# Where PReLU reads its product: PSUM or the scaled copy in SBUF

## The chip, the cores and the metric

The kernel runs on one core of one Trainium2 chip. The metric is the device time of one execution in microseconds. The core's engines are TensorE (PE in the profile; PEld is its weight load), VectorE (DVE), ScalarE (ACT), GpSimd (POOL) and SyncE (SP, which only issues DMAs here). They run side by side; each works through its own instructions in a fixed order and waits on semaphores for the others.

## The reference

An attention over pooled keys and values, and behind it a feed-forward layer with a PReLU:

```python
k_p = k.reshape(B, H, Sp, 8, D).mean(axis=3)          # B 8, H 8, S 576, D 64, Sp 72
v_p = v.reshape(B, H, Sp, 8, D).mean(axis=3)
scores = scale * np.matmul(q, k_p.transpose(0, 1, 3, 2))
attn = softmax(scores)
x = np.matmul(attn, v_p)                               # to 4608 x 512
h = x @ w_in                                           # 512 -> 2048
g = np.maximum(h, 0.0) + alpha * np.minimum(h, 0.0)    # alpha: one per column of h
out = g @ w_out                                        # 2048 -> 512
```

All inputs and outputs are fp32.

## The kernel before

The 4608 tokens are cut into 9 chunks of 512 (`CH`). Each chunk passes through attention (scores, softmax, a transpose by DMA, the product with v), through FFN1 and through FFN2. FFN1 has 16 slices of 128 hidden columns (`NF`), FFN2 has 4 tiles of 128 tokens (`TPC`). To keep the precision of fp32, each operand of a product is split into a high and a low fp16 part and three matmuls are made of one: L766 to L768 in FFN1, L813 to L815 in FFN2.

One slice `f` of FFN1 goes from engine to engine:

1. `ffn1_products` (TensorE): 12 matmuls of 128x512 into one PSUM bank `h`. There are two such banks (`ps_h`, `bufs=2`), so slice f+2 can start only when the bank of slice f has been read for the last time.
2. `ffn1_scaled` (ScalarE, L772): t = h * rp, from PSUM to an fp32 tile in SBUF.
3. `ffn1_prelu` (VectorE, L776): t = max(h * ra, t). It reads h from PSUM and t from SBUF.
4. `ffn1_parts` with l = 0 (ScalarE, L784): the high fp16 part of t.
5. `ffn1_parts` with l = 1 (GpSimd, L787): the low part, t minus the high part; then g is ready for FFN2.

`rp` and `ra` hold one factor per hidden column: rp is a scale with the sign that makes the maximum right, and ra is rp * alpha. `al` holds alpha itself. All three are written once, in the opening stage.

The opening stage (`start`, some 160 us) also loads, scales and splits the weights. It contains chunk 0 with an order on all engines that is written out by a planner (`_Plan`, with ranks in `RK`) and fixed under `manual_schedule`. From chunk 1 on the order on each engine is chosen by the framework's own scheduler, from the order of the program, the dependences between the tiles and a timeline of its own. In the program, the attention of chunk c+1 is spread over the FFN1 slices of chunk c: k and q scales (the small VectorE operations at L212, L217, L233, L238), the split of k and q (L426, L429, L442, L446), softmax (L511 to L547), the transposes, and the sums over 8 values of v on GpSimd (L467). FFN2 steps of the same chunk may run between FFN1 slices as far as their g is ready.

Of the kernel before, what the change touches and what calls it, by code (L numbers as in the profile page):

```python
# [136 lines left out]
def pooled_attention_prelu_ffn(ctx: ExitStack, tc: tile.TileContext, qT, kT, vT, kN, vN, w1, w2, alpha, out):  # L137
# [5 lines left out]
    nc = tc.nc  # L143
# [38 lines left out]
    al = const.tile([P, NF], F32, name="al")  # L182
# [574 lines left out]
    gs, hps, hs = {}, {}, {}  # L757
# [14 lines left out]
        nc.scalar.activation(t, hps[c, f], AF.Copy, scale=rp[:, f:f + 1])  # L772

    def ffn1_prelu(c, f):
        t = hs[c, f]
        nc.vector.scalar_tensor_tensor(out=t, in0=hps.pop((c, f)), scalar=ra[:, f:f + 1], in1=t,  # L776
                                       op0=ALU.mult, op1=ALU.max)

    def ffn1_parts(c, f, l):
# [46 lines left out]
    def start():  # L826
# [35 lines left out]
        for f in range(NF):  # L862
            rank = due[1](f)
            if f:
                x = add("PE", 2.59, lambda f=f: ffn1_products(0, f), wd[1, f], first, rank=rank, take="h")
            else:
                x = wd[1, f]
                for n in range(NK):
                    x = add("PE", 0.64, lambda n=n: ffn1_products(0, 0, slice(n, n + 1)), x, xd[n],
                            rank=rank, take=None if n else "h")  # L870
                first = x
            x = add("ACT", 0.69, lambda f=f: ffn1_scaled(0, f), x, rs[f], rank=rank + RK["sc"], take="f")
            x = add("DVE", 0.76, lambda f=f: ffn1_prelu(0, f), x, rank=rank + RK["pre"], give="h")
            rd.append(x)
            x = add("ACT", 0.62, lambda f=f: ffn1_parts(0, f, 0), x, rank=rank + RK["hi"])
            gd.append(add("Pool", 1.2, lambda f=f: ffn1_parts(0, f, 1), x, rank=rank + RK["lo"], give="f"))
# [34 lines left out]
    for c in range(1, NC):  # L911
        line = _Line()
        if c + 1 < NC:
            attention(line.add, c + 1, _new_b(c + 1), 0.0)
        mixes = 5 * (NPR // 2)
        n = -(-(len(line.ops) - mixes) // (NF - 2))
        for f in range(NF):
            ffn1_products(c, f)
            ffn1_scaled(c, f)
            ffn1_prelu(c, f)  # L920
            ffn1_parts(c, f, 0)
            ffn1_parts(c, f, 1)
            with (tc.issue_after(last["t"].ins), tc.issue_after(last["x"].ins), tc.issue_after(last["xh"].ins),
                  tc.issue_after(last["o"].ins)):
                line.emit(min(n, len(line.ops) - mixes))
        for i in range(TPC):
            ffn2(c, i)
            if i == 1:
                line.emit(mixes)
# [32 lines left out]
```

## Time and profile before

| | |
|---|---|
| median of 3 runs | 902.24 us (900.93 to 907.07) |
| profiled execution | 903.4 us |
| span of its instructions | 901.7 us |
| mean granted TensorE clock | 0.985 |
| TensorE matmul busy | 846.9 us (94% of the span) |
| ScalarE busy | 430.6 us (48%) |
| VectorE busy | 407.2 us (45%) |
| GpSimd busy | 347.8 us (39%) |

A line of the page's groups reads: source line, engine, operation, what it writes and reads by the program's names, shapes, how many; then busy time, mean ns of one, the engine's idle time just before them, and what ended most of it. A line of the waits reads: who waited, on what; total us, times, longest. In the timeline the first number is the start in us from the span's beginning and the second the length in us; rows of one kind that follow each other are merged (x2). Matmuls are pipelined, so that a matmul of 0.38 us is followed by the next after a shorter time.

### The profile page before, as it was taken

How to read it: one execution, taken by the hardware profiler on the slowest of the kernel's cores; microseconds unless marked ns; L12 is line 12 of the kernel's file. 1: busy time of each engine (PE TensorE's matmuls, PEld its weight loads, DVE VectorE, ACT ScalarE, POOL GpSimd, SP SyncE). 2: the span in 40 equal slices, each digit the busy share in tenths (PEclk: the TensorE clock that was granted, in tenths of full speed). 3: DMA queues.
4: the chain of work that ended last, by engine and by line, in shares of the span. 5: the costliest groups of instructions: out<-in, count | busy, mean ns of one | idle time of the engine just before them, and what ended most of it. 6: DMA issues, size and time to landing. Idle time of an engine off the chain costs nothing.

```text
span 901.7 us, 11443 instructions
## 1 busy us (share of the span) xinstructions
PE 846.9 (94%) x4404; PEld 405.8 (45%) x4404; DVE 407.2 (45%) x657; ACT 430.6 (48%) x727; POOL 347.8 (39%) x375
## 2 busy tenths in 40 slices
PE   5779899989898989999989999999989999999998
PEld 4444354444344444454435444544444444444443
DVE  4889895484128520762077116621572145111110
ACT  5899984555324631563246234632464346313330
POOL 1357364376214730564055504640455027302320
PEclk9889999999999999999999999999999999999999
DMA  9686033606210360045012601260115004000000
GB/s 331 218 264 257 25 86 65 198 4 156 87 51 4 71 172 24 27 74 172 24 27 51 172 36 39 48 175 36 39 27 117 36 13 77 18 35 12 1 23 25
DMA packets 93638, 74.73 MB, mean 83 GB/s; under 512 B 77040, under 2 KB 77616, under 8 KB 93584
## 3 DMA queue, kind: packets, MB, share of 16 engines
q1 hardware_dynamic: 93584, 74.01, 29.2%
q8 instruction: 34, 0.56, 0.3%
q14 instruction: 20, 0.16, 0.1%
HBM read 45.10 MB, written 9.44 MB: 60 GB/s over the span
## 4 chain that ended last, share of the span: by engine, by line
PE 65%; DVE 11%; issue 7%; ACT 6%; DMA 6%; POOL 4%; SPq 1%; POOLq 0%; DVEq 0%; ACTq 0%
PE o L813 10%; PE o L814 10%; PE o L815 10%; PE h L766 9%; PE h L767 9%; PE h L768 9%; DMA vraw<-vT_dram 3%; POOL g L787 3%; DVE t L776 2%; DVE e L233 2%; DVE q L446 1%; PE x L609 1%; DMA nat<-kN_dram 1%; SPq L254 1%; ACT q L442 1%
## 5 line engine op out<-in xcount | busy, mean ns | idle before, releaser
L787 POOL TENSOR_TENSOR g<-t,g 128x512 f16<-128x512 f32 x144 | 166.9, 1160 | 397.7 <-ACT g L784 393.4
L776 DVE SCALAR_TENSOR_TENSOR t<-h,m,t 128x512 f32<-128x512 f32 x144 | 107.0, 744 | 308.4 <-ACT t L772 303.7
L766 PE MATMUL h<-x,w 128*128 128x512 f16 x576 | 220.0, 384 | 17.2 <-DVE t L776 13.9
L767 PE MATMUL h<-x,w 128*128 128x512 f16 x576 | 221.2, 384 | 0.0
L768 PE MATMUL h<-x,w 128*128 128x512 f16 x576 | 221.1, 384 | 0.0
L813 PE MATMUL o<-w,g 128*128 128x512 f16 x544 | 206.1, 380 | 10.7 <-POOL g L787 10.5
L814 PE MATMUL o<-w,g 128*128 128x512 f16 x544 | 206.4, 379 | 0.0
L815 PE MATMUL o<-w,g 128*128 128x512 f16 x544 | 204.4, 380 | 0.0
L772 ACT ACTIVATE t<-h,rp 128x512 f32<-128x512 f32 x144 | 97.5, 682 | 117.4 <-PE h L768 96.2
L784 ACT CAST g<-t 128x512 f16<-128x512 f32 x144 | 88.6, 615 | 99.0 <-DVE t L776 98.3
L803 ACT ACTIVATE o<-o,os 128x512 f32<-128x512 f32 x34 | 23.1, 687 | 156.3 <-PE o L815 156.3
L767 PEld LDWEIGHTS <-w 128*128 128x128 f16 x576 | 56.9, 99 | 83.4 <-issue 23.9
L813 PEld LDWEIGHTS <-g 128*128 128x128 f16 x576 | 56.3, 98 | 79.7 <-POOL g L787 13.1
L768 PEld LDWEIGHTS <-w 128*128 128x128 f16 x576 | 57.0, 99 | 69.7 <-issue 3.5
L815 PEld LDWEIGHTS <-g 128*128 128x128 f16 x576 | 56.4, 98 | 67.8 <-issue 0.3
L766 PEld LDWEIGHTS <-w 128*128 128x128 f16 x576 | 56.5, 99 | 65.9 <-issue 4.0
L814 PEld LDWEIGHTS <-g 128*128 128x128 f16 x576 | 56.4, 98 | 65.0 <-issue 0.6
L467 POOL TENSOR_TENSOR vraw<-vraw 72x512 f32<-72x512 f32 (+1 forms) x56 | 53.7, 972 | 43.0 <-DMA vraw<-vT_dram 39.2
L570 DVE SCALAR_TENSOR_TENSOR x<-x,xsc,x 128x512 f16<-128x512 f32 x36 | 26.1, 748 | 65.5 <-ACT x L566 65.5
L536 POOL TENSOR_TENSOR e<-e,sm 128x576 f32<-128x576 f32 x35 | 40.5, 1158 | 34.6 <-DVE sm L534 33.6
L541 ACT CAST apad<-e 128x576 f16<-128x576 f32 x72 | 44.9, 669 | 14.6 <-POOL e L536 12.4
L544 POOL TENSOR_TENSOR apad<-e,apad 128x448 f16<-128x448 f32 x36 | 37.3, 1035 | 17.7 <-ACT apad L541 17.6
(135 smaller groups left out, 840.6 us busy)
## 6 DMA issues: line engine op xcount, KB each, us to landing
w<-w_dram SPq DMA_DIRECT2D x16, 1024.0 KB
out_dram<-o SPq DMA_DIRECT2D x36, 256.0 KB
qraw<-qT_dram SPq DMA_DIRECT2D x17, 512.0 KB
vraw<-vT_dram SPq DMA_DIRECT2D x28, 288.0 KB
kraw<-kT_dram SPq DMA_DIRECT2D x12, 576.0 KB
kq<-kT_dram SPq DMA_DIRECT2D x2, 576.0 KB
nat<-kN_dram SPq DMA_DIRECT2D x2, 512.0 KB
nat<-vN_dram SPq DMA_DIRECT2D x2, 512.0 KB
```

The costliest lines, as they stand in the source:

```text
L467: nc.gpsimd.tensor_tensor(out=o, in0=y, in1=z, op=ALU.add)
L541: x = add("ACT", 0.67, lambda l=l, ap=ap, ev_=ev_: nc.scalar.copy(out=ap[:, l, :, :SP], in_=ev_()), x, *td[i - 2:i - 1], rank=rk)
L766: nc.tensor.matmul(ps, w[:, 1, ks_], x[:, 0], start=(n == 0), stop=False)
L767: nc.tensor.matmul(ps, w[:, 0, ks_], x[:, 1], start=False, stop=False)
L768: nc.tensor.matmul(ps, w[:, 0, ks_], x[:, 0], start=False, stop=(n == NK - 1))
L772: nc.scalar.activation(t, hps[c, f], AF.Copy, scale=rp[:, f:f + 1])
L776: nc.vector.scalar_tensor_tensor(out=t, in0=hps.pop((c, f)), scalar=ra[:, f:f + 1], in1=t, op0=ALU.mult, op1=ALU.max)
L784: nc.scalar.copy(out=g[:, 0], in_=t)
L787: nc.gpsimd.tensor_tensor(out=g[:, 1], in0=t, in1=g[:, 0], op=ALU.subtract)
L813: nc.tensor.matmul(ps, g[:, 1, ts_], w[:, 0], start=(f == 0), stop=False)
L814: nc.tensor.matmul(ps, g[:, 0, ts_], w[:, 1], start=False, stop=False)
L815: nc.tensor.matmul(ps, g[:, 0, ts_], w[:, 0], start=False, stop=(f == NF - 1))
```

## The change

In chunk 0 nothing changes. In chunks 1 to 8 the PReLU multiplies the scaled copy t by alpha instead of multiplying h by rp * alpha: max(t * al, t) with t = h * rp is the same value. The first input of the instruction is then t in SBUF and no longer h in PSUM; both its tensors lie in SBUF, and the scaled copy is the last instruction that reads the bank h.

```diff
     def ffn1_prelu(c, f):
-        t = hs[c, f]
-        nc.vector.scalar_tensor_tensor(out=t, in0=hps.pop((c, f)), scalar=ra[:, f:f + 1], in1=t,
+        t, h = hs[c, f], hps.pop((c, f))
+        nc.vector.scalar_tensor_tensor(out=t, in0=t if c else h, scalar=(al if c else ra)[:, f:f + 1], in1=t,
                                        op0=ALU.mult, op1=ALU.max)
```

## The prediction

> **What bounds the kernel now.** I read the page's busy times first, then its costliest groups, then the waits of TensorE, and then went down to single instructions in the timeline.
>
> ```profile
> PE 846.9 (94%) x4404; PEld 405.8 (45%) x4404; DVE 407.2 (45%) x657; ACT 430.6 (48%) x727; POOL 347.8 (39%) x375
> ...
> L776 DVE SCALAR_TENSOR_TENSOR t<-h,m,t 128x512 f32<-128x512 f32 x144 | 107.0, 744 | 308.4 <-ACT t L772 303.7
> ```
>
> TensorE is busy for 94% of the span; VectorE, which runs the changed PReLU (L776, 144 times 744 ns), has more than half of it free. So the change can pay only where TensorE stands still, or cost only where it makes TensorE stand still. The waits of TensorE from 160 us to the end, that is after the opening stage:
>
> ```profile
> PE h L766 <- DVE t L776: 12.9, 7, 2.6
> PE o L813 <- POOL g L787: 10.5, 6, 3.4
> ```
>
> Columns: total us, times, longest. Seven waits, 12.9 us together, are the first matmul of an FFN1 slice (L766) waiting for a PReLU to give back one of the two h banks. Six more, 10.5 us, are FFN2 waiting for a g from GpSimd. The same view over one chunk at a time (160 to 205 us, then to 300, 390, 480, 570, 660) shows where the seven lie:
>
> ```profile
> PE h L766 <- DVE t L776: 1.6, 1, 1.6
> PE h L766 <- DVE t L776: 2.7, 2, 2.3
> PE h L766 <- DVE t L776: 1.8, 1, 1.8
> PE h L766 <- DVE t L776: 2.6, 1, 2.6
> PE h L766 <- DVE t L776: 1.8, 1, 1.8
> PE h L766 <- DVE t L776: 2.3, 1, 2.3
> ```
>
> One long wait per chunk, always at the same place, some 10 us into FFN1 of chunks 1 to 6; the remaining 0.4 us of the second row is a short one. Here is one of them in the timeline (first start, then length, in us; ScalarE, VectorE, GpSimd, TensorE):
>
> ```profile
> 373.63 2.19 ACT L442 ACTIVATE q<-qraw,s 128x1024 f16<-128x1024 f32 x2
> 375.72 1.24 ACT L772 ACTIVATE t<-h,rp 128x512 f32<-128x512 f32 x2
> ...
> 367.72 1.01 DVE L217 TENSOR_SCALAR pr<-pt 128x3 f32<-128x3 f32 x1
> 368.65 0.74 DVE L776 SCALAR_TENSOR_TENSOR t<-h,m,t 128x512 f32<-128x512 f32 x1
> 369.31 2.79 DVE L233 TENSOR_SCALAR e<-pr 128x3 int32<-128x3 int32 x1
> ...
> 374.81 2.48 DVE L446 SCALAR_TENSOR_TENSOR q<-qraw,s,q 128x1024 f16<-128x1024 f32 x2 [0.37 <-ACT q L442]
> 377.21 0.74 DVE L776 SCALAR_TENSOR_TENSOR t<-h,m,t 128x512 f32<-128x512 f32 x1
> ...
> 367.44 1.84 POOL L467 TENSOR_TENSOR vraw<-vraw 72x512 f32<-72x512 f32 x2
> 369.24 1.15 POOL L787 TENSOR_TENSOR g<-t,g 128x512 f16<-128x512 f32 x1
> 370.35 0.61 POOL L467 TENSOR_TENSOR vraw<-vraw 72x256 f32<-72x256 f32 x1
> 370.92 1.16 POOL L787 TENSOR_TENSOR g<-t,g 128x512 f16<-128x512 f32 x1
> ...
> 375.78 0.38 PE L815 MATMUL o<-w,g 128*128 128x512 f16 x1
> 378.01 0.38 PE L766 MATMUL h<-x,w 128*128 128x512 f16 x1 [1.85 <-DVE t L776]
> 380.59 0.22 PE L209 MATMUL pm<-pd,ones 128*128 128x128 bf16 x1
> ```
>
> The reader is to see the order of events. A tiny VectorE operation on 128x3 (L233) is stretched to 2.79 us while GpSimd runs without a break from 367.44 to 372.08. That holds the scales back, so ScalarE reaches its two q copies late, and the two scaled copies (L772) stand behind those. VectorE then makes the two q products (L446) and only then the PReLU (377.21 to 377.95). TensorE starts at 378.01, straight after it, and the 12 matmuls of the slice last until 380.59: 2.58 us a slice, 0.215 a matmul.
>
> **The change part by part.**
>
> *The early release.* After the change the PReLU no longer reads h, so the last reader of an h bank is the scaled copy on ScalarE. In the rows above the first of the two copies ends half way through the pair, at 375.72 + 0.62 = 376.34, and TensorE's last matmul before the wait is over at 375.78 + 0.38 = 376.16. The wait would shrink from 1.85 us to about 0.25: 377.95 - 376.34 = 1.6 us off. Applied to the five waits of 1.8 to 2.6 us this is 5 x 1.6 = 8.0; the waits of 1.6 and 0.4 us go altogether, 2.0. Sum: **-10.0 us**. Bounds: nothing, if the freed bank is found late for another reason, and -12.9, all seven. What is late next is the scaled copy itself, behind q.
>
> *The clock after a wait.* Behind the 2.6 us wait FFN1 matmuls start 0.42 us apart, twice the 0.215 above:
>
> ```profile
> 471.79 0.63 PE L768 MATMUL h<-x,w 128*128 128x512 f16 x1
> 472.21 0.63 PE L766 MATMUL h<-x,w 128*128 128x512 f16 x1
> ```
>
> The stretches of that chunk and of the one before it (the sixth figure after a stretch's length is the granted clock):
>
> ```profile
> 300.00:390.00 90.00, 85.73 (x450) 40.51 (x448) 35.30 (x56) 38.65 (x63) 35.77 (x40) 1.00 0.28 70
> 390.00:480.00 90.00, 86.30 (x443) 40.61 (x442) 38.09 (x59) 37.14 (x61) 33.68 (x37) 0.98 0.29 74
> ```
>
> The clock is 0.98 in the chunk with the 2.6 us wait, which is 0.02 x 90 = 1.8 us, and 1.00 in the chunk with the 1.85 us one. If the long waits shrink below 1 us, the 1.8 comes back; a second chunk with a wait near that length might give as much. I take **-2**, bounds 0 and -4.
>
> *The PReLU's operands.* It still has 128x512 fp32 elements and one instruction; only in0 moves from PSUM to SBUF. The trace has no such PReLU, but it has neighbours:
>
> ```profile
> L691 DVE SCALAR_TENSOR_TENSOR w<-v,s,w x16: 700/746/1757, 105.1 to 147.1; 128x512 f16<-128x512 f32 x16
> L776 DVE SCALAR_TENSOR_TENSOR t<-h,m,t x144: 692/750/779, 67.6 to 872.7; 128x512 f32<-128x512 f32 x144
> L663 DVE SCALAR_TENSOR_TENSOR v<-w,v x2: 1212/1218/1224, 24.1 to 68.3; 128x1024 int32<-128x1024 int32 x2
> L663 DVE SCALAR_TENSOR_TENSOR v<-w,vw x14: 1208/1214/1247, 51.0 to 144.5; 128x1024 int32<-128x1024 int32 x14
> ```
>
> The same instruction with both tensors in SBUF (L691) has a median of 746 ns, against 750 for the PReLU (min/median/max). With two 32-bit SBUF inputs (L663 from v) it takes 1218 ns per 1024 elements, with one of them in PSUM (from vw) 1214. So the bare cost is unchanged: 0, bounds -50 to +50 ns, hidden under TensorE either way.
>
> *The contention.* The maximum of L691 is 1757 ns, while the PReLU's is 779. The row behind it, and what GpSimd ran at that time:
>
> ```profile
> 118.46 1.76 DVE L691 SCALAR_TENSOR_TENSOR w<-v,s,w 128x512 f16<-128x512 f32 x1
> ```
>
> ```profile
> 117.77 2.91 POOL L467 TENSOR_TENSOR vraw<-vraw 72x512 f32<-72x512 f32 x2 [1.48 <-DMA vraw<-vT_dram]
> ```
>
> With two SBUF inputs the instruction waited about 1.0 us for the GpSimd addition under way, and the two additions, about 1.27 us each when alone (1.84 less 0.61 in the rows above), took 2.91 together, 0.4 us more. The Trainium skill, "SBUF — State Buffer", section "Who interferes with whom", says this in general: a VectorE instruction with two SBUF inputs contends with a GpSimd instruction that reads SBUF, and the second to start waits; one SBUF input does not. It speaks against this change, and the two maxima agree with it. Met at random, a PReLU finds GpSimd at work with its share of a chunk, 35.77 of 90 us, or 0.40, and then waits half a GpSimd operation, 0.58 us: 0.23 us each, 16 x 0.23 = 3.7 us per chunk on an engine that is free for 55 of 90. Only what reaches TensorE counts. That is the stage before the long wait: the PReLU at 368.65 now holds GpSimd's 0.61 us addition by up to 0.74 us, GpSimd's streak ends that much later, and L233 with it. The bounds are +0.7 per chunk, and -2 if L233 gets its turn while GpSimd is held. I take +0.5 x 6 chunks = **+3**, bounds -12 and +4.
>
> *Queues behind it.* ScalarE's cast (L784) waits for the PReLU, and the next scaled copy, which now frees the bank, stands behind that cast:
>
> ```profile
> ACT g L784 <- DVE t L776: 98.3, 101, 2.5
> ```
>
> 101 times ScalarE already stands there. A PReLU that is 0.23 us late passes that on to the copy. The cover is the second bank: one slice of FFN1, 2.58 us. Without cover it would be 96 x 0.23 = 22 us in chunks 1 to 6. I take **+1**. The waits for g are put down to GpSimd's queue, whose own wait there is for the vraw load; the PReLU is long over by then, so I leave those 10.5 us.
>
> Sum: -10 - 2 + 3 + 1 = -8 against the profiled execution's 903.4 us (span 901.7 and 1.7 around it): **895.4, say 895 us**. The median of the three runs, 902.24, is 1.2 lower, so this is -0.8%; about 1% is what a measurement of this kernel can tell from no change. One more uncertainty is in every term: from chunk 1 on, the order on each engine is chosen by the framework from the dependences, and the change alters one. Chunk 0 keeps its order and its PReLU.
>
> **The rivals.**
>
> 1. *No change.* The wait changes hands: the scaled copies stand behind the q copies (2.19 us in the row at 373.63), so TensorE waits for ScalarE instead, or the order just spends the freed bank on running into the g wait sooner. For it: both waits come from a chunk of work that arrives late on in-order engines. Against: in the row the copy ends 1.6 us before the PReLU. -10 is then cancelled: 902. This is also how the change would fail to do what it says.
>
> 2. *Much faster.* With banks free, FFN1 runs through and TensorE keeps FFN2 work in hand for the moment when g is late. Then 12.9 us and, say, half of 10.5 go, with 2 of clock: 903.4 - 20 = 883.
>
> 3. *Slower.* Place: the FFN1 stage of chunks 1 to 6, where GpSimd runs softmax and v sums back to back. Mechanism: a PReLU held behind GpSimd holds the cast, the cast holds the scaled copy, the copy holds the bank. It decides as soon as the hold and what stood there before pass the 2.6 us of the second bank; L233's 2.79 us shows that a streak can do that. Price: the early release gains nothing, and each chunk pays one GpSimd operation (1.16 us) and a third of the clock's 1.8 us: 6 x 1.76 = 10.6, so 914. Against: an instruction of this kind got its turn after one GpSimd operation at 118.46.
>
> 4. *Halved rate.* The Trainium skill, "Vector Engine (DVE) Microarchitecture Reference", section "7. Points that are easy to get wrong", says that this instruction with two non-bf16 SBUF sources runs at half throughput. L663 does not agree (1218 against 1214 ns). As a mechanism here: a PReLU as long as L446's (2.48 / 2 = 1.24 us), +0.5 us each; a chunk's 8 us still lie under TensorE, and about +0.5 per chunk reaches it: 898.
>
> **How the numbers follow.** Forecast 0.40, no change 0.25, much faster 0.15, slower 0.16, halved rate 0.04. Around each I allow 6 us for the new order. The forecast then falls below 893 one time in three, the much faster case always: 0.13 + 0.15, with 0.05 from the others 0.33. Above 911 lie two thirds of the slower case, 0.11, and a little of the others, together 0.14. The rest is 0.53. Leaving out half of the much faster case and half of the slower one gives 882 to 914.
>
> **What would show it.** In the profile after, TensorE's waits on the PReLU should be gone outside chunk 0, with waits of under 1 us on the scaled copy at most; the PReLU's maximum should rise from 779 ns to 1.5 to 2 us with a median near 750; GpSimd's L787 should average more than the 1.15 us of the rows above; the granted clock should be 1.00 in the chunk of 390 to 480. Were the median near 1.2 us, rival 4 holds. If TensorE waits on the scaled copy for as long as it waited on the PReLU, rival 1; if the cast's wait of 98 us rises by tens of us and TensorE's with it, rival 3. An order that moves softmax or v work against FFN1 would make the working wrong, whatever the sign.

## The result, and the profile after

The changed kernel takes 873.38 us (median of 4 runs, 871.39 to 876.16) against 902.62 us: a ratio of 0.967, 95% interval 0.963 to 0.972. Measured again (e11 below) the ratio is 0.966 (0.963 to 0.969). The change is worth 29 us where 8 were forecast, and 873 lies below the range of 882 to 914. One of the ten runs of e1 below, the profiled one, took 1266.6 us at a granted clock of 0.66 and is left out of e1's figures.

TensorE's busy row, and the groups of PReLU and of GpSimd's low part, in the profile after:

```profile
PE 840.7 (96%) x4404; PEld 406.4 (46%) x4404; DVE 425.9 (49%) x657; ACT 428.8 (49%) x727; POOL 367.1 (42%) x375
...
L787 POOL TENSOR_TENSOR g<-t,g 128x512 f16<-128x512 f32 x144 | 174.5, 1213 | 362.1 <-ACT g L784 359.5
L776 DVE SCALAR_TENSOR_TENSOR t<-t,al 128x512 f32<-128x512 f32 x128 | 125.1, 979 | 272.3 <-ACT t L772 261.6
```

PReLU in chunks 1 to 8 became slower, 979 ns on average where it took 744, and GpSimd's L787 too, 1213 ns for 1160. Yet TensorE's waits from 160 us on have nearly gone:

```profile
PE h L766 <- ACT t L772: 2.5, 1, 2.5
PE h L766 <- ACT o L803: 1.4, 1, 1.4
PE o L813 <- ACT o L803: 0.2, 1, 0.2
```

That is the whole list: 4.1 us. Before it was 12.9 + 10.5, and 1.6 in these last two rows as well: 25.0 us. So 20.9 us of the 27.3 by which the span shrank are waits of TensorE, and both kinds have gone, the waits for PReLU and those for g. The clock gives part of the rest. Behind 160 us it drops in three short stretches before and in one after, and is 1.00 between them (the sixth figure behind the length is the granted clock):

```profile
235.00:239.50 4.50, 4.50 (x14) 1.71 (x15) 0.75 (x1) 2.91 (x6) 0.51 (x1) 0.62 0.31 117
283.00:287.50 4.50, 4.50 (x24) 2.29 (x22) 1.29 (x5) 1.50 (x3) 2.25 (x3) 0.62 0.00 0
471.00:475.00 4.00, 4.00 (x16) 1.66 (x15) 0.66 (x2) 1.05 (x3) 2.31 (x2) 0.57 0.02 4
```

```profile
190.00:194.50 4.50, 3.97 (x12) 1.44 (x12) 3.30 (x5) 2.67 (x5) 1.73 (x2) 0.62 0.02 4
```

Each costs some 1.7 us (0.38 of 4.5, 0.43 of 4.0), so the clock gives 5.1 - 1.7 = 3.4 us. Each follows a long wait: 3.4 us for g and 2.3 and 2.6 us for PReLU before, 2.5 us for the scaled copy after. Not every wait of that length does it: behind 2.4 us for g, at 332 us before, the clock stays at 1.00. Waits and clock make 24.3 of the 27.3 us; the other 3 were not traced.

What the prediction did not have in its sum is the second thing that changed: the order on the engines. FFN2 matmuls fill the gaps of FFN1. The first of their three lines, in FFN1 of chunk 3, before (356 to 416.3 us) and after (345 to 399.5 us):

```profile
L813 PE MATMUL o<-w,g 128*128 128x512 f16 x23 | 8.7, 379 | 0.0
```

```profile
L813 PE MATMUL o<-w,g 128*128 128x512 f16 x17 | 6.4, 379 | 0.0
```

Counted in TensorE's order of instructions over all three lines, out of 192 FFN2 matmuls per chunk, 62 to 78 came before the end of the chunk's FFN1, in chunks 1 to 8; after the change it is 46 to 51, and 66 in the last. More FFN2 work is in hand when FFN1 ends.

### The profile page after: what moved, and what is told of

The parts are those of the page before. It is cut to its first block, busy times and chain, and to the rows that moved or that the text cites. A ratio compares the mean times of both kernels' runs of the same rounds, so it can differ in the third digit from the quotient of the medians.

```text
span 874.4 us, 11435 instructions
## 1 busy us (share of the span) xinstructions
PE 840.7 (96%) x4404; PEld 406.4 (46%) x4404; DVE 425.9 (49%) x657; ACT 428.8 (49%) x727; POOL 367.1 (42%) x375
## 4 chain that ended last, share of the span: by engine, by line
PE 85%; DVE 6%; ACT 4%; DMA 2%; issue 1%; SPq 1%; POOL 0%; ACTq 0%; POOLq 0%
PE o L813 13%; PE o L815 13%; PE o L814 13%; PE h L766 13%; PE h L768 13%; PE h L767 13%; PE x L609 2%; DMA nat<-kN_dram 1%; PE s L598 1%; PE s L599 1%; DVE t L776 1%; PE s L600 1%; DMA qraw<-qT_dram 1%; DVE m L242 1%; PE h L815 1%
## 5 line engine op out<-in xcount | busy, mean ns | idle before, releaser
L787 POOL TENSOR_TENSOR g<-t,g 128x512 f16<-128x512 f32 x144 | 174.5, 1213 | 362.1 <-ACT g L784 359.5
L776 DVE SCALAR_TENSOR_TENSOR t<-t,al 128x512 f32<-128x512 f32 x128 | 125.1, 979 | 272.3 <-ACT t L772 261.6
L813 PE MATMUL o<-w,g 128*128 128x512 f16 x544 | 205.8, 379 | 0.3 <-ACT o L803 0.2
L784 ACT CAST g<-t 128x512 f16<-128x512 f32 x144 | 88.6, 615 | 99.9 <-DVE t L776 99.5
L813 PEld LDWEIGHTS <-g 128*128 128x128 f16 x576 | 56.3, 98 | 68.6 <-issue 1.5
L467 POOL TENSOR_TENSOR vraw<-vraw 72x512 f32<-72x512 f32 (+1 forms) x56 | 55.5, 1008 | 46.8 <-DMA vraw<-vT_dram 32.4
L536 POOL TENSOR_TENSOR e<-e,sm 128x576 f32<-128x576 f32 x35 | 44.5, 1273 | 19.6 <-DVE sm L534 19.6
L544 POOL TENSOR_TENSOR apad<-e,apad 128x448 f16<-128x448 f32 x36 | 39.4, 1095 | 14.8 <-ACT apad L541 14.6
```

Source lines behind the costliest of these rows:

```text
L467: nc.gpsimd.tensor_tensor(out=o, in0=y, in1=z, op=ALU.add)
L776: nc.vector.scalar_tensor_tensor(out=t, in0=t if c else h, scalar=(al if c else ra)[:, f:f + 1], in1=t, op0=ALU.mult, op1=ALU.max)
L784: nc.scalar.copy(out=g[:, 0], in_=t)
L787: nc.gpsimd.tensor_tensor(out=g[:, 1], in0=t, in1=g[:, 0], op=ALU.subtract)
L813: nc.tensor.matmul(ps, g[:, 1, ts_], w[:, 0], start=(f == 0), stop=False)
```

## The experiments

Two theories. **R**: the early release of the bank saves the time, as in the prediction's sum. **O**: the new order saves it; on the chip itself the early release matters little. To tell them apart, I took the order apart from the operands. The instructions have the same numbers in both kernels, so an order can be laid down as edges of issue order, which make no engine wait for another (shortened, marked by "..."; e1 lays down the list "PE" alone):

```diff
+ORDER = {"PE": "...", "DVE": "...", "Activation": "...", "Pool": "..."}   # numbers of instructions, in order
+def pin_order(nc, tc):
+    made = {i.name: i for i in nc.cur_bb.bb.instructions}
+    for ids in ...:
+        for a, b in zip(ids, ids[1:]):
+            tc.add_manual_dep(made[f"I-{b}"], f"I-{a}", mybir.DependencyInfo(
+                mybir.DependencyClass.NoSync, mybir.DependencyReason.DATA), reason="order")
```

**e1, new operands in the old order.** The changed kernel with TensorE's order of before laid down; the other engines then had their old orders too.

> The changed PReLU, but every engine works through chunks 1 to 8 in the order that it had before the change. The h bank is free after the scaled copy, nothing else differs. Theory R (the early release as such pays, by the prediction's sum): the waits for PReLU fall from 12.9 us to under 4, the 10.5 us of waits for g stay, about 893 to 896 us. Theory O (the new order pays, the bank's earlier release on the chip matters little): 898 to 904 us.

Measured: 0.999 (0.996 to 1.002), 902.08 us (median of nine). With the old order the change does nothing that can be measured.

**e2, old operands in the new order.** The kernel before with the order of the changed one laid down on four engines.

> The old PReLU, which reads h from PSUM and holds the bank, but every engine works through chunks 1 to 8 in the order of the changed kernel. Theory O: the waits for g vanish, since FFN1 runs ahead and FFN2 work is left for when g is late; some waits for PReLU remain; 876 to 886 us. Theory R: without the early release TensorE waits in this order for PReLU in most slices of FFN1, 895 us or more.

Measured: 873.50 us, 0.967 (0.964 to 0.971), a little better than even theory O had it. The order alone gives the whole gain, with the PReLU that holds the bank. TensorE's waits from 160 us on (L869 is the first FFN1 line here, L879 PReLU):

```profile
PE h L869 <- DVE t L879: 2.0, 2, 1.0
PE h L869 <- ACT o L906: 1.4, 1, 1.4
```

Waits for PReLU fall from 12.9 to 2.0 us although it still gives back the bank; no wait for g is left. Theory R is out as an account of the 29 us.

**e3, two SBUF inputs, bank held, old order.** The changed kernel in the old order, and behind the PReLU:

```diff
...
+        if c:
+            nc.vector.tensor_copy(out=held, in_=h[:, :1])     # held: 128x1 in SBUF
```

> The changed PReLU with the order of before on every engine, and behind each PReLU VectorE copies one column of h, so that the bank is held as long as before. What is left of the change is that PReLU has two SBUF inputs and can meet GpSimd. The prediction's contention terms, with no gain against them: 903 to 908 us. If contention costs nothing that reaches TensorE: 901 to 904 us. PReLU's mean should be near 980 ns, as in the changed kernel.

Measured: 920.58 us, 1.019 (1.014 to 1.024), 17 us more. The cost is far above the forecast, although PReLU's mean is 831 ns and not the 980 expected. The waits (L896 is GpSimd's low part, L886 the copy that holds the bank):

```profile
PE o L922 <- POOL g L896: 18.0, 7, 4.8
PE h L873 <- DVE held L886: 17.0, 8, 3.1
```

Both kinds have grown, 10.5 to 18.0 and 12.9 to 17.0. The copy itself takes 0.15 us each time and can have a part in both; what it adds was not measured apart, so the 17 us are not the price of the contention alone.

**e4, one SBUF input, new order.** The changed kernel in its own order, with

```diff
+            nc.vector.tensor_reduce(out=t, in_=t.rearrange("p (a b) -> p a b", b=1), axis=AX.X, op=ALU.max)
```

in place of PReLU in chunks 1 to 8; the product with alpha and the maximum are left out there.

> The order of the changed kernel on every engine, early release too, but in chunks 1 to 8 the PReLU is replaced by a VectorE reduction over groups of one element, from t to t, with one SBUF input and the same 128x512 elements: the product with alpha and the maximum are left out there. It should not meet GpSimd: near 750 ns with a maximum under 0.8 us. If contention costs the changed kernel what the prediction took (3 to 4 us), this runs at 869 to 871 us; if contention stays hidden, 872 to 875 us.

Measured: 870.80 us, 0.964 (0.961 to 0.968). That lies in the range expected for a contention that costs 3 to 4 us. By the medians it is 2 to 3 us below the changed kernel (873.38, 872.48 in e11), which the intervals do not tell from nothing: in the new order contention costs 0 to 3 us. The substitute, at most 687 ns long, does not meet GpSimd:

```profile
L880 DVE TENSOR_REDUCE t<-t 128x512 f32<-128x512 f32 x128 | 87.0, 681 | 292.9 <-ACT t L875 279.1 <-POOL g L893 7.6 <-issue 5.9
```

The substitute is also 63 ns shorter than PReLU before (744 - 681), so this is an upper bound on what contention costs there.

**e5, e1's profile.**

> The kernel with the changed PReLU in the old order once more, for the waits behind its time, which lay within 0.4% of the kernel before. Early release and contention cancel: waits of TensorE for PReLU gone, some 5 us of new waits for the scaled copy, and waits for g above 10.5 us, 16 to 18 as with the bank held. If neither does anything: the waits of the kernel before.

Measured: 899.26 us in one run. TensorE's waits from 160 us on, and PReLU (L813 is here the first FFN1 line, L819 the scaled copy, L823 PReLU, L834 the low part):

```profile
PE o L860 <- POOL g L834: 15.0, 7, 4.2
PE h L813 <- ACT t L819: 6.5, 6, 1.9
...
L823 DVE SCALAR_TENSOR_TENSOR t<-t,al 128x512 f32<-128x512 f32 x128 | 111.7, 874 | 303.3 <-ACT t L819 296.5 <-issue 4.0 <-POOL apad L594 2.7
```

The release works: 12.9 us of waits for PReLU became 6.5 us for the scaled copy. But the waits for g grew from 10.5 to 15.0 us. So e1 stands at 0.999 because two effects cancel, and not because neither is there.

**e6, the early release alone, old order.** The same reduction as in e4, in the old order.

> The old order on every engine and the early release, with the reduction over groups of one element in place of PReLU in chunks 1 to 8 (product with alpha and maximum left out), which should not meet GpSimd. This is the early release alone. The prediction's first term: 10 us off, 12 with the clock, 889 to 893 us. If the release is worth in this order what separates the held from the released bank with two SBUF inputs (18 us): 883 to 886. If it is worth nothing without a new order: 899 to 903.

Measured: 888.34 us, 0.985 (0.980 to 0.990), 14 us off, near the first of the three cases. The waits:

```profile
PE o L922 <- POOL g L896: 8.9, 6, 2.7
PE h L872 <- ACT t L878: 2.7, 3, 1.3
```

So in the old order the release is worth 14 us, and contention (e1 less e6, 0.999 less 0.985) takes 13 of them back. As in e4, the shorter substitute makes both figures upper bounds.

**e7 and e8, all FFN2 work kept in stock.** What in the new order pays? One candidate is the stock of FFN2 work at the end of FFN1. Its extreme:

```diff
-            nc.tensor.matmul(ps, w[:, 0, ks_], x[:, 0], start=False, stop=(n == NK - 1))
+            last["h"] = nc.tensor.matmul(ps, w[:, 0, ks_], x[:, 0], start=False, stop=(n == NK - 1))
...
         for i in range(TPC):
-            ffn2(c, i)
+            with tc.issue_after(last["h"].ins):
+                ffn2(c, i)
```

At that point `last["h"]` is the chunk's last FFN1 matmul.

e7 in the kernel before:

> The kernel before with one edge of issue order: no FFN2 matmul of a chunk is issued before the last FFN1 matmul of that chunk. If the new order pays because FFN2 work is kept in stock for the end of FFN1, when g and the product with v are late, the waits for g vanish here too, but FFN1 has no filler while PReLU holds the banks: waits for PReLU of 2 to 4 us per chunk, 880 to 895 us. If the order pays through something else, waits of more than 25 us in all, over 900.

e8 in the changed kernel:

> The changed kernel with the same edge: no FFN2 before the end of FFN1. With the bank free after the scaled copy FFN1 needs little filler: 870 to 880 us, no waits for g. If fillers are needed while VectorE and ScalarE work on k and q at the chunk's start, waits for the scaled copy of some 3 us per chunk bring it to 885 to 895.

Measured: e7 941.76 us, 1.043 (1.039 to 1.046); e8 913.84 us, 1.012 (1.009 to 1.016). Both expectations missed: the times were far too low. By the letter e7 fell into the case of "something else" (over 900 us), but the waits for g went as its first case has it. The waits on PReLU in e7, and on the scaled copy in e8:

```profile
PE h L766 <- DVE t L776: 51.9, 19, 7.6
```

```profile
PE h L766 <- ACT t L772: 28.3, 9, 6.9
```

In neither is a wait for g left. A full stock ends those, as thought, but with no FFN2 filler FFN1 stands still, above all where ScalarE and VectorE are busy with k and q: 52 us in all with the bank held by PReLU, 28 with the early release. One wait of 5.8 to 7.6 us at that place in each of chunks 1 to 6 makes up 37 of the 52.

**e9, some stock.** The kernel before, with FFN2 of the second token tile stopped at step 4 until FFN1 is over. The first part of FFN1 keeps its filler:

```diff
...
         for f in range(NF):
-            ffn2_step(c, i, f, ps)
+            if i == 1 and f == 4:
+                with tc.issue_after(last["h"].ins):
+                    ffn2_step(c, i, f, ps)
+            else:
+                ffn2_step(c, i, f, ps)
```

> The kernel before with one edge of issue order: step 4 of FFN2's second token tile, and so all later steps of it, is not issued before the last FFN1 matmul of the chunk. By the issue orders, 51 FFN2 matmuls of a chunk then come before the end of FFN1 (62 to 76 before, 46 to 51 in the changed kernel), and the first part of FFN1 keeps its 24. If the stock left at the end of FFN1 is what ends the waits for g: they fall from 10.5 us to under 3, the waits for PReLU stay near 13 or grow by a few us; 888 to 896 us. If the waits for g depend on something else: 900 or more.

Measured: 889.73 us, 0.985 (0.982 to 0.988), as expected. The waits:

```profile
PE h L766 <- DVE t L776: 11.4, 7, 2.3
...
PE o L813 <- POOL g L787: 0.6, 1, 0.6
```

The waits for g depend on the stock, and one edge per chunk nearly ends them with the old PReLU: 13 to 15 us, the 10 us of waits and some clock. (With the edge the framework also moved a few instructions on the other engines; their part was not tried alone.) That is about half of the 29 us. The waits for PReLU stay here at 11.4 us, where the new order has 2.0 (e2); what in the order ends those, no run isolates.

**e10 and e11, the change in chunk 0 too.**

```diff
-        nc.vector.scalar_tensor_tensor(out=t, in0=hps.pop((c, f)), scalar=ra[:, f:f + 1], in1=t,
+        nc.vector.scalar_tensor_tensor(out=t, in0=t, scalar=al[:, f:f + 1], in1=t,
...
-            x = add("ACT", 0.69, lambda f=f: ffn1_scaled(0, f), x, rs[f], rank=rank + RK["sc"], take="f")
-            x = add("DVE", 0.76, lambda f=f: ffn1_prelu(0, f), x, rank=rank + RK["pre"], give="h")
+            x = add("ACT", 0.69, lambda f=f: ffn1_scaled(0, f), x, rs[f], rank=rank + RK["sc"], take="f", give="h")
+            x = add("DVE", 0.76, lambda f=f: ffn1_prelu(0, f), x, rank=rank + RK["pre"], two=True)
```

> The changed kernel with chunk 0 changed as well: its PReLU takes t and alpha, its bank is given back by the scaled copy, and the planner is told both. The waits for PReLU in chunk 0 are some 2 us and the planner makes a new order of the opening stage: 870 to 880 us; a gain beyond 2 us is not expected, a loss of 5 us is possible because VectorE and GpSimd are at their busiest there.

> The changed kernel itself on the chip of these runs, to stand beside the two others: 871 to 876 us.

Measured on one chip: e10 881.19 us, 0.975 (0.971 to 0.979), a loss of 9 us where at most 5 were thought possible; e11, the changed kernel, 872.48 us. Chunk 0 is better left alone. The first scaled copy of chunk 1, in e10 and in e11:

```profile
172.48 0.69 ACT L772 ACTIVATE t<-h,rp 128x512 f32<-128x512 f32 x1 [1.03 <-PE h L768]
```

```profile
164.73 0.69 ACT L772 ACTIVATE t<-h,rp 128x512 f32<-128x512 f32 x1 [1.16 <-PE h L768]
```

The opening stage is 7.8 us longer in e10; from there on e10 is no slower in these two profiles. Whether contention or the plan's ranks do it was not tried apart.

## Why the prediction was wrong

**The step that failed is the one on the order**: "Around each I allow 6 us for the new order", and before it the sentence that leaves the 10.5 us of waits for g as they are. The order was no noise around a sum. It was the change: e2 has 29 us from it with nothing else changed, and e1 without it has nothing. The reason that held g's waits fixed (its queue waits for a vraw load) names what is late, not what TensorE has to do meanwhile; e9 shows that this decides. The second rival had the mechanism, with half of the g waits, no credit for the order at the chunk's start, and 0.15 of the chance.

That the framework counts the bank as free earlier, and so spends less filler on FFN1, fits the issue orders: the kernel of e3 without a laid-down order (built, not run), whose PReLU has the new operands and whose bank is held, gets 62 to 78 FFN2 matmuls before the end of FFN1, the range of before the change. So it is the released bank that leads the framework to the new order, not the operand.

**The early release, -10, and the clock, -2**: right in mechanism and nearly in size, if the order stays and nothing meets GpSimd: e6 measures -14, and in its profile the waits for the bank fall by 12.9 - 2.7 = 10.2 us. The clock gives 3.4 us in the changed kernel, inside the bounds of 0 to 4. What is late next is the scaled copy, as forecast, with those 2.7 us.

**The contention, +3, and the queues behind it, +1**: mis-sized for the old order. It takes up to 13 us there (e1 against e6), and 17 with the bank held and the copy (e3). The guess of 0.23 us per PReLU was not too low; in e5 it is 874 - 744 = 0.13 us. What the sum lacked is where it lands: the waits for g, which the sum held fixed, are 8.9 us in e6 and 15.0 in e5, and those for the scaled copy 2.7 and 6.5. That the meetings fall where GpSimd works without a break and TensorE is out of filler, so that an average can't price them, is argued and not shown meeting by meeting. In the new order PReLU loses more, 0.24 us each in the changed kernel (979 - 744), and it costs 0 to 3 us. ScalarE's cast, by which the queues were to pass the delay on, waits 99.5 us in the changed kernel for 98.3 before.

By its own terms, then, the prediction's 895 us belongs to a kernel in the old order, and that one takes 899 to 902.

Two readings in the working were off, and no term hangs on either. The two additions at 117.77 are, like the pair at 367.44, one of 72x512 and one of 72x256, which take 1.84 us together when undisturbed; at 2.91 us GpSimd lost 1.07 us in that stretch, not 0.4. And the long waits lie later in FFN1 than some 10 us: the one at 378.01 lies 22 us behind the start at 356 us.

**The operands at no cost**: right. PReLU's minimum and median with two SBUF inputs:

```profile
L776 DVE SCALAR_TENSOR_TENSOR t<-t,al x128: 734/752/3431, 166.4 to 843.5; 128x512 f32<-128x512 f32 x128
```

The median was 750. The halved rate (the fourth rival, and the sentence of the Trainium skill's "Vector Engine (DVE) Microarchitecture Reference", section "7. Points that are easy to get wrong") does not occur with two fp32 SBUF inputs. The maximum, 3431 ns, is beyond the 1.5 to 2 us expected. L787's growth came (1160 to 1213 ns), but the order has a part in it: e2, with the old operands, has 1188. The end of TensorE's waits for PReLU after chunk 0 came too, though for the order's sake, as e2 shows; the one wait left for the scaled copy is 2.5 us, where less than 1 was expected.

**The slower rival**: a cost of that kind is real, as e3's +1.9% shows, but it came out as a loss only in the old order with a held bank.

## What to carry to other kernels

Where a scheduler makes the order, an edit that changes a dependence is first of all a new order, and its price can't be read from the old trace wait by wait. Ask what filler the bound engine will have left at each late arrival, and measure order and edit apart, by laying the old order over the new kernel and the new one over the old. Filler work is a stock: spent early it covers early waits, kept it covers late ones. Keeping all of it made each of the two kernels some 40 us slower here (e7, e8); how much to keep had to be tried.

## What the runs showed of the hardware

A VectorE instruction with two SBUF inputs does not always get its turn when the GpSimd operation under way ends. One PReLU of the changed kernel, and GpSimd at that time:

```profile
355.77 2.37 DVE L776 SCALAR_TENSOR_TENSOR t<-t,al 128x512 f32<-128x512 f32 x1 [1.79 <-ACT t L772]
```

```profile
355.22 1.15 POOL L787 TENSOR_TENSOR g<-t,g 128x512 f16<-128x512 f32 x1
356.33 1.27 POOL L467 TENSOR_TENSOR vraw<-vraw 72x512 f32<-72x512 f32 x1
357.56 1.06 POOL L467 TENSOR_TENSOR vraw<-vraw 72x256 f32<-72x256 f32 x1
```

L787 ends at 356.37; the PReLU ends at 358.14, so with its 0.75 us it ran from about 357.4, near the end of the next GpSimd operation. It let that one pass, although that one started 0.56 us later than the PReLU. In these rows GpSimd's next operation starts 0.04 us before the last is over; whether this is the reason is not shown. The addition on 72x256 behind them took 1.06 us, where it takes 0.61 alone.

The small VectorE operation on 128x3 (L233) is held by such streaks too, though it reads one tensor only, and how often it meets one is again a matter of order. Its mean before, after the change, and in e2 (ns, second figure behind the bar):

```profile
L233 DVE TENSOR_SCALAR e<-pr 128x3 int32<-128x3 int32 x7 | 14.7, 2095 | 0.1
```

```profile
L233 DVE TENSOR_SCALAR e<-pr 128x3 int32<-128x3 int32 x7 | 5.9, 842 | 0.2
```

```profile
L336 DVE TENSOR_SCALAR e<-pr 128x3 int32<-128x3 int32 x7 | 3.9, 560 | 0.2
```

In e2 nothing but the order differs from the kernel before, and this operation takes less than a third of the time. Part of the delay only moves: the scale operation behind it (L238, L341 in e2) takes 867 ns there for 422 before. How much of the 12.9 us of waits at the chunks' starts went through this, and how much through the stock of FFN2 work there, was not separated.
